# Channel-mix groups of four chunks, weights standing in all three products, and small copies on ScalarE's queue, in a fused attention and channel-mix kernel

## The chip, the cores and the metric

The kernel runs on one core of a Trainium2 chip. The metric is the device time of one execution in microseconds (us); the kernel before has a median of 341.86 us over 3 runs (341.74 to 342.92). The engines are named as the profile names them: PE is TensorE (matmuls; PEld is its weight load), ACT is ScalarE, DVE is VectorE, POOL is GpSimd, and SP is the queue that issues most transfers (DMAs). An instruction that issues a DMA stands in an engine's own queue, in order with its other instructions.

## The reference

Two stages, all in float32. The first is a gated linear attention over 768 steps, for 4 batches of 8 heads with 48 features; the second mixes channels of the result (384 features, 1024 hidden).

```python
for t in range(S):                      # S = 768, per batch and head
    state = alpha[t][:, None] * state + outer(k[t], v[t])
    y[t] = q[t] @ state
x = y, heads side by side               # (4, 768, 384)
x_prev = x shifted by one step, zero at the start of each batch
xk = mu_k * x + (1 - mu_k) * x_prev;  xr = mu_r * x + (1 - mu_r) * x_prev
k = relu(xk @ w_k);  v = (k * k) @ w_v;  r = sigmoid(xr @ w_r)
out = r * v
```

## The kernel before

**Chunks.** The 4 x 768 steps are 24 chunks of 128 steps, six to a batch. For the attention the chunks are prepared in groups (`PREP`, 2 2 2 3 3 3 3 3 3): for a group, the decays (`al`) are multiplied up by two scans on DVE (`scan` L823, `scan_back` L840), the queries and keys (one tile `kq`) are scaled with them (`mul_q` L848, `mul_k` L853), and the rows of the fourth pair of heads are copied to a tile of their own, `kq3`, by four DMAs (`move` L868). Then every chunk has a "visit" on PE: scores (L969), transposes (L986), the chunk's own part of y (L1017), the update of the state (L1029) and, one visit later, the part of y from the state (L1043). ACT copies y out of PSUM (`copy_y` L1088), and two DMAs per chunk spread the rows of the fourth pair over the other tiles (`move_y3` L1097).

**Groups of the channel mix.** `MIX` has the groups 2 2 2 3 3 3 3 3 3. For a group of n columns (256 or 384 steps) ACT and DVE form xk and xr from the tile `xt` (`x_mul` L1125, `x_add` L1129) and split each into a high part in the reduced format fp32r and a low remainder (`x_hi` L1134, `x_lo` L1138). Every product of the channel mix is then three matmuls: high by high, low by high, high by low. In `up` (L1154) the weights stand in the array and x streams through: 8 pieces of 9 matmuls, n columns each. `relu` and the square follow on ACT and DVE, and k is split again (L1183, L1187). In `gate` (L1198) and `down` (L1221) it is the other way round: x or k stands, 128 steps at a time, and 384 columns of weights stream through, so a group of c chunks has c x 9 and c x 24 matmuls. `sigmoid` (L1206), `gated` (L1228) and `store` (L1232) end a block of 128 steps by 384 features. Group 0 runs unsplit in float32, where PE works through two instructions per matmul.

**Buffers.** `kq` has two buffers, so the load for preparation group g (counted from 0) waits until group g-2 is read: group 2 waits for group 0, group 3 for group 1. The weights are loaded in ten pieces, put together on ACT and DVE (L911, L920), and split into high and low parts for group 1 on (L929, L931, L935). PSUM holds two accumulators for the channel mix (`pm`).

**Order.** A planner in the program (`Plan`, `graph`) lays out all work before the kernel runs: a table of numbers (`SOONER`) moves a step's rank on its engine, and `SPOTS` says before which piece of the channel mix each attention visit stands on PE. The order of every engine and queue is then fixed; an instruction waits for those before it. All the small copies (`move`, `move_y3`) stand in SP's queue, between the loads and the stores:

```python
iq, mq = dma(2, L("move", g, Q_AT), mulq + scales + old + [zeroed[g % 2]], ...)
_, x = dma(2, L("move_y3", c), es, kb=rows_kb(NX, C * 4, 6))
```

Before the first channel-mix matmul PE runs filler matmuls that compute nothing that is used (`busy` L952).

Of the kernel before, what the change touches and what calls it, by code (L numbers as in the profile page):

```python
# [42 lines left out]
MIX = [2, 2, 2, 3, 3, 3, 3, 3, 3]  # L43
# [41 lines left out]
class Plan:  # L85
# [33 lines left out]
    def run(self, order, sooner):  # L119
# [39 lines left out]
        dma, end = self.FIRST + 1.1, 0.0  # L159
# [79 lines left out]
def PLACE_OF(c):  # L239
# [1228 lines left out]
```

## Time and profile before

| | |
|---|---|
| median of 3 runs | 341.86 us (341.74 to 342.92) |
| the profiled execution, its own time | 343.06 us |
| its span (first to last instruction) | 341.3 us |
| PE busy | 326.9 us, 96% of the span, 4552 instructions |
| DVE busy | 241.8 us, 71% |
| ACT busy | 193.9 us, 57% |
| moved by DMA | 35.38 MB |

The profile shows one execution. A row of a timeline or of the chain of waits has its start and its length in us from the start of the span. In brackets stands how long the engine was idle before an instruction, and which engine and tile ended that. PE's matmuls overlap one another and their ends are modelled, so the pace of a run of matmuls is read from the chain of waits (length by count) and not from the mean duration of one. PEclk 1.00 is the upper of TensorE's two clock levels, 2.4 GHz.

### The profile page before, as it was taken

The numbers are of one execution on the slowest core, as the hardware profiler recorded it, in microseconds if no ns is written. First come the engines' busy times: TensorE is split into PE (matmuls) and PEld (weight loads), VectorE is DVE, ScalarE is ACT, GpSimd is POOL, SyncE is SP. The second block draws the span as 40 slices with busy tenths as digits, with TensorE's granted clock in tenths as the row PEclk, the third lists the DMA queues.
The fourth block names the chain that finished last, engine by engine and source line by source line (L and its number), as shares of the span: only waits on it lengthen the run. The fifth ranks groups of instructions, "written<-read, shape, count | busy, mean of one in ns | idle before, by whom it ended". The sixth has DMA issues, their size and how long they took to land.

```text
span 341.3 us, 10699 instructions
## 1 busy us (share of the span) xinstructions
PE 326.9 (96%) x4552; PEld 307.8 (90%) x4552; DVE 241.8 (71%) x513; ACT 193.9 (57%) x439; POOL 7.4 (2%) x28
## 2 busy tenths in 40 slices
PE   8889899899999999999999999999999999999992
PEld 8778765689999999999999999999999999999991
DVE  4899996989984998796769955885642784187210
ACT  3497882588388478653765456654641875366300
POOL 5100000000000000000000000000000000000000
PEclk9999999999999999999999999999999999999997
DMA  8999673434425322441241405130000100010010
GB/s 216 405 340 268 198 257 128 128 99 152 127 52 205 78 74 85 147 124 51 84 146 19 135 32 179 45 69 37 8 10 19 43 24 8 31 46 2 2 46 30
DMA packets 14325, 35.38 MB, mean 104 GB/s; under 512 B 2432, under 2 KB 9344, under 8 KB 13504
## 3 DMA queue, kind: packets, MB, share of 16 engines
q1 hardware_dynamic: 14016, 33.73, 30.5%
q10 hardware_dynamic: 256, 0.92, 0.9%
q8 instruction: 37, 0.61, 0.7%
q14 instruction: 16, 0.13, 0.1%
HBM read 26.57 MB, written 4.72 MB: 92 GB/s over the span
## 4 chain that ended last, share of the span: by engine, by line
PE 84%; DMA 6%; DVE 5%; issue 1%; ACT 1%; DVEq 0%
PE pk L1154 28%; PE pv L1221 27%; PE pg L1198 10%; PE yu L1043 4%; DMA kq<-kq_p 4%; PE sp L969 3%; PE yu L1017 3%; PE sp L986 3%; PE yu L1029 3%; DMA al<-al_p 2%; PE pb L952 2%; DVE pp L840 2%; DVE kq L848 1%; DVE pp L823 1%; DVE kq L853 0%
## 5 line engine op out<-in xcount | busy, mean ns | idle before, releaser
L1221 PE MATMUL pv<-wvh,kh 128*128 128x384 f32 x176 | 59.7, 339 | 0.2 <-DVE flag L1250 0.2
L1221 PE MATMUL pv<-wvh,kl 128*128 128x384 f32 x176 | 59.3, 337 | 0.0
L1221 PE MATMUL pv<-wvl,kh 128*128 128x384 f32 x176 | 59.2, 337 | 0.0
L1154 PE MATMUL pk<-xkh,wkh 128*128 128x384 f32 (+1 forms) x192 | 42.3, 327 | 1.0 <-ACT x L1125 0.7
L1162 ACT ACTIVATE r<-pk 128x384 f32<-128x384 f32 (+1 forms) x72 | 32.4, 451 | 18.9 <-PE pk L1154 18.7
L1154 PE MATMUL pk<-xkl,wkh 128*128 128x384 f32 (+1 forms) x192 | 41.5, 325 | 0.0
L1187 DVE TENSOR_TENSOR kl<-k,kh 128x384 fp32r<-128x384 f32 (+1 forms) x64 | 33.4, 523 | 11.3 <-ACT k L1168 4.8
L1154 PE MATMUL pk<-xkh,wkl 128*128 128x384 f32 (+1 forms) x192 | 41.0, 322 | 0.0
L1170 DVE TENSOR_TENSOR k<-r 128x384 f32<-128x384 f32 x48 | 26.7, 557 | 13.8 <-ACT r L1162 13.1
L1183 ACT ACTIVATE kh<-r 128x384 fp32r<-128x384 f32 (+2 forms) x72 | 35.1, 489 | 2.0
L1154 PEld LDWEIGHTS pk<-xkh,wkh 128*128 128x128 f32 x192 | 32.2, 188 | 1.9 <-ACT x L1125 1.3
L1221 PEld LDWEIGHTS pv<-wvh,kh 128*128 128x128 f32 x176 | 33.0, 188 | 0.5 <-DVE flag L1250 0.3
L1125 ACT ACTIVATE x<-xt,mu 128x384 f32<-128x384 f32 (+1 forms) x48 | 26.3, 583 | 12.4 <-DVE xkl L1138 6.3
L1221 PEld LDWEIGHTS pv<-wvl,kh 128*128 128x128 f32 x176 | 33.0, 188 | 0.0
L1221 PEld LDWEIGHTS pv<-wvh,kl 128*128 128x128 f32 x176 | 33.0, 188 | 0.0
L1154 PEld LDWEIGHTS pk<-xkh,wkl 128*128 128x128 f32 x192 | 32.4, 188 | 0.0
L1154 PEld LDWEIGHTS pk<-xkl,wkh 128*128 128x128 f32 x192 | 32.0, 188 | 0.0
L1228 DVE TENSOR_TENSOR sig<-pv,sig 128x384 f32<-128x384 f32 x24 | 13.3, 553 | 24.6 <-PE pv L1221 24.5
L1129 DVE SCALAR_TENSOR_TENSOR x<-xt,nu,x 128x384 f32<-128x384 f32 (+1 forms) x48 | 26.5, 576 | 4.5 <-ACT x L1125 4.5
L1088 ACT COPY xt<-yu 48x256 f32<-48x256 f32 (+1 forms) x72 | 26.8, 372 | 4.8 <-PE yu L1043 3.4
L992 ACT COPY ht<-sp 128x288 f32<-128x288 f32 (+1 forms) x24 | 9.7, 403 | 34.2 <-PE sp L986 19.2
L977 DVE TENSOR_TENSOR am<-sp,mask 128x512 f32<-128x512 f32 x24 | 16.5, 689 | 16.2 <-PE sp L986 9.0
(89 smaller groups left out, 535.4 us busy)
## 6 DMA issues: line engine op xcount, KB each, us to landing
kq<-kq_p SPq DMA_DIRECT2D x6, 1153.5 KB, 5.8
out<-sig SPq DMA_DIRECT2D x24, 192.0 KB, 1.9
al<-al_p SPq DMA_DIRECT2D x6, 577.5 KB, 3.9
v<-v_p SPq DMA_DIRECT2D x6, 576.0 KB, 4.0
rk<-wk_p SPq DMA_DIRECT2D x4, 768.0 KB, 9.0
rv<-wv_p SPq DMA_DIRECT2D x4, 768.0 KB, 5.3
kq<-kq_p SPq DMA_DIRECT2D x2, 769.5 KB, 8.1
v<-v_p SPq DMA_DIRECT2D x3, 384.0 KB, 7.6
```

The lines of the kernel that those rows point to most:

```text
L977: self.DVE.tensor_tensor(am, self.sc_both.rearrange("k j (p t) -> k j p t", p=NP), self.mask.unsqueeze(1).unsqueeze(1).to_broadcast([C, 2, ...
L1043: self.PE.matmul(self.yu[c][at : at + D, s, p * HB : (p + 1) * HB], self.st[c, s][rows, p, :], self.kq_of(c, p, j, Q_AT, s), start=False, ...
L1088: self.ACT.copy(self.xt_of(m)[dst, :, at + s * HB : at + (s + 1) * HB], self.yu[c][src, s, : NP * HB].rearrange("r (p t) -> r p t", p=NP),)
L1125: self.ACT.activation(x, xt[:, t, 1 : 1 + n], AF.Copy, scale=self.mu[:, i, t : t + 1])
L1129: self.DVE.scalar_tensor_tensor(x, xt[:, t, 0 : xt.shape[2] - 1], self.nu[:, i, t : t + 1], x, op0=ALU.mult, op1=ALU.add)
L1154: self.PE.matmul(pk, w[:, t, f * 128 : (f + 1) * 128], x[:, t], start=part == 0 and t == 0, stop=part == len(pairs) - 1 and t == NT - 1,)
L1162: self.ACT.activation(self.r[m, f], pk, AF.Relu)
L1170: self.DVE.tensor_tensor(k2, r, r, op=ALU.mult)
L1183: self.ACT.activation(self.khl_of(m)[0][:, f], self.r[m, f], AF.Square)
L1187: self.DVE.tensor_tensor(kl[:, f], self.k2[m, f], kh[:, f].bitcast(F32), op=ALU.subtract)
L1198: self.PE.matmul(pg, x[:, i, t * 128 : (t + 1) * 128], w[:, i], start=part == 0 and i == 0, stop=part == len(pairs) - 1 and i == NT - 1,)
L1221: self.PE.matmul(pv, x[:, f, cols], w, start=f == 0 and i == 0, stop=f == NF - 1 and i == len(pairs) - 1,)
```

## The change

- The last 12 chunks form three groups of four instead of four groups of three (`MIX`), so 512 columns stream per matmul there. Such a group may lie across the end of a batch; then its `xt` has two spans. Its x and k tiles take memory that the weights' pieces leave (`late_tiles`), and its temporary x uses `tops`.
- In `gate` and `down` the weights stand and x or k streams. The result has features on its rows, so the output is stored as (384, 3072) and turned on the host.
- The four copies per preparation group and the two per chunk are issued from ACT's queue.
- Preparation group 1's `kq` lies where the low part of the down weights comes later (tag `wvl`). Group 2's load thus waits for no earlier group, group 3's for group 0 and not for group 1; the low down weights wait for group 1's last use.
- `r` and its square share one tile (three buffers), so `k_hi` follows the square; the square is on ACT in group 1 only, before in groups 1 and 2.
- `SPOTS` and the table `SOONER` are new.

```diff
-MIX = [2, 2, 2, 3, 3, 3, 3, 3, 3]
+MIX = [2, 2, 2, 3, 3, 4, 4, 4]
+LATE = [m for m, cs in enumerate(MG) if len(cs) > 3]
+def spans_of(m):
+    cs = MG[m]
+    n = 2 if any(c % NCB == 0 for c in cs[1:]) else 1
+    return n, len(cs) * C // n
...
 SPOTS = [
-    0, 0, 0, 0, 0, 0, 0, 0, 0, 0, 0, 0, 0, 2, 3, 3, 5, 7, 8, 8, 15, 21, 27, 33, 59, 65, 71, 100,
+    0, 0, 0, 0, 0, 0, 0, 0, 0, 0, 0, 0, 0, 3, 5, 7, 10, 11, 12, 14, 14, 23, 29, 34, 68, 74, 81,
...
-        old = uses[("kq", g - 2)] if g > 1 else []
+        old = uses[("kq", g - 2 if g > 3 else 0)] if g > 2 else []
...
-        iq, mq = dma(2, L("move", g, Q_AT), mulq + scales + old + [zeroed[g % 2]], kb=rows_kb(NX, n * 4, 6))
-        ik, mk = dma(2, L("move", g, K_AT), mulk + old + [zeroed[g % 2]], kb=rows_kb(NX, n * 4, 6))
+        iq, mq = dma(2, L("move", g, Q_AT), mulq + scales + old + [zeroed[g % 2]], kb=-rows_kb(NX, n * 4, 6), eng="ACT")
+        ik, mk = dma(2, L("move", g, K_AT), mulk + old + [zeroed[g % 2]], kb=-rows_kb(NX, n * 4, 6), eng="ACT")
...
-                _, x = dma(2, L("move_y3", c), es, kb=rows_kb(NX, C * 4, 6))
+                _, x = dma(2, L("move_y3", c), es, kb=-rows_kb(NX, C * 4, 6), eng="ACT")
...
-            self.kq[g] = self.p2.tile([rows_of(g), nt, w], F32, tag="kq", name=f"kq{g}")
+            pool, tag = (self.p1, "wvl") if g == 1 else (self.p2, "kq")
+            self.kq[g] = pool.tile([rows_of(g), nt, w], F32, tag=tag, name=f"kq{g}")
...
+        if m in LATE:
+            self.ACT.copy(xt[dst, :, cols], y[:, :NT])
+            self.ACT.copy(y3[dst, :, cols], y[:, NT:])
...
+    def late_tiles(self):
+        if not self.late:
+            self.late = [self.p1.tile([128, 3, LONG], F32R, tag=f"raw{i}", name=f"late{i}") for i in range(3)]
+        return self.late
...
+        elif m in LATE:
+            x = self.tops[(NT * i + t) % 2].bitcast(F32)[:, :LONG]
...
-    def gate(self, m, t, part):
+    def gate(self, m, e, part):
...
             self.PE.matmul(
-                pg, x[:, i, t * 128 : (t + 1) * 128], w[:, i],
+                pg, w[:, i, e * 128 : (e + 1) * 128], x[i],
...
-    def down(self, m, t, f0):
+    def down(self, m, e, f0):
...
                 self.PE.matmul(
-                    pv, x[:, f, cols], w,
+                    pv, w, x[f],
...
-        self.queue[eng].dma_start(self.out[at : at + C], self.sig.pop((m, t)))
+        self.queue[eng].dma_start(self.out[e * 128 : (e + 1) * 128, at : at + sig.shape[1]], sig)
```

SP's queue early in the program, before: `kq_481` and `kq_769` are the keys and queries of preparation groups 2 and 3, `rv` pieces of the down weights, `al` decays, `kq_1_81` and `kq_0_80` the tiles for the fourth pair, `xt` the input of the channel mix.

```order
L868 DMA kq_1_81<-kq_165 48x1x256 x2
L879 DMA rv_460<-wv_p 128x3072
L812 DMA kq_481<-kq_p 128x1539
L879 DMA rv_587<-wv_p 128x3072
L868 DMA kq_0_80<-kq_481 48x1x257 x2
L806 DMA al_640<-al_p 128x1155
L868 DMA kq_0_80<-kq_481 48x1x256 x2
L1097 DMA xt_448<-xt_448 16x3x128 x2
L879 DMA rv_702<-wv_p 128x3072
L816 DMA v_711<-v_p 128x1152
L812 DMA kq_769<-kq_p 128x2307
L1097 DMA xt_448<-xt_448 16x3x128 x2
```

SP's queue now, from the keys of group 1 (`kq_171`) on; `kq_177` are those of group 2, `kq_415` those of group 3, `rk` and `rr` pieces of the up and gate weights.

```order
L841 DMA kq_171<-kq_p 128x1539
L841 DMA kq_177<-kq_p 128x1539
L834 DMA al_212<-al_p 128x771
L908 DMA rk_289<-wk_p 128x3072
L908 DMA rr_300<-wr_p 128x3072
L908 DMA rr_352<-wr_p 128x1536
L845 DMA v_361<-v_p 128x768
L841 DMA kq_415<-kq_p 128x2307
L834 DMA al_447<-al_p 128x771
L908 DMA rv_454<-wv_p 128x3072
L908 DMA rv_474<-wv_p 128x3072
```

Group 2's load now follows group 1's directly, ahead of the pieces of the gate weights; group 3's stands ahead of all pieces of the down weights and no longer behind them; no small copy is left in between.

ACT's queue before, from the copies of chunk 1's y (`xt_144<-yu`) to the first `relu` (`r<-pk`); `xkh<-xt_144` forms the first input of the channel mix, `tops` belongs to putting a weight piece together.

```order
L1088 COPY xt_144<-yu 48x4x64 x2
L911 ACTIVATE tops_85<-rk_285 128x768
L911 ACTIVATE tops_84<-rr_297 128x768
L911 ACTIVATE tops_85<-rr_345 128x384
L1125 ACTIVATE xkh<-xt_144,mu 128x256 x3
L1125 ACTIVATE xrh<-xt_144,mu 128x256 x3
L911 ACTIVATE tops_84<-rv_430 128x768
L1162 ACTIVATE r<-pk 128x256
```

ACT's queue now, over the same stretch (`junk` is a check of the decays that stood ahead of the copies before).

```order
L1134 COPY xt_110<-yu 48x4x64 x2
L888 ACTIVATE junk,racc<-al_212,mone 128x768
L1141 DMA xt_110<-xt_110 16x3x128 x2
L940 ACTIVATE tops_88<-rk_289 128x768
L897 DMA kq_1_84<-kq_171 48x1x257 x2
L940 ACTIVATE tops_87<-rr_300 128x768
L1202 ACTIVATE xkh<-xt_110,mu 128x256 x2
L940 ACTIVATE tops_88<-rr_352 128x384
L1202 ACTIVATE xkh<-xt_110,mu 128x256
L1202 ACTIVATE xrh<-xt_110,mu 128x256
L897 DMA kq_1_84<-kq_171 48x1x256 x2
L1202 ACTIVATE xrh<-xt_110,mu 128x256 x2
```

Six issues, chunk 1's copies and the four of group 1, now stand between the copy of y and the first `relu`, two pairs of them and the piece `rr_300` ahead of the first input.

## Rows read from the trace of the kernel before

**Rows 1.** Busy time by stage, from the windows view (length, then each engine)
```profile
0.00:28.77 28.77, 24.84 (x387) 23.07 (x387) 22.15 (x56) 16.21 (x28) 6.15 (x21) 1.00 0.91 315
28.77:71.45 42.68, 39.07 (x549) 28.45 (x547) 38.41 (x83) 27.47 (x65) 0.19 (x1) 1.00 0.56 181
60.00:110.00 50.00, 48.15 (x949) 44.48 (x949) 43.15 (x98) 36.03 (x101) 0.10 (x1) 1.00 0.42 130
71.45:334.80 263.35, 263.04 (x3619) 256.24 (x3619) 180.66 (x375) 150.21 (x348) 1.02 (x6) 1.00 0.23 70
```

**Rows 2.** The chain that ended last: start, length, step, and its count
```profile
28.93 2.60 PE pk L1154 x12
31.53 5.89 DMA kq<-kq_p
...
48.60 7.44 DMA kq<-kq_p
...
61.20 4.68 DMA al<-al_p
...
78.47 3.18 PE pk L1154 x27
81.65 3.32 PE pg L1198 x18
84.97 8.32 PE pv L1221 x48
...
215.43 4.76 PE pg L1198 x27
220.19 12.72 PE pv L1221 x72
...
304.13 12.49 PE pk L1154 x72
```

**Rows 3.** PE's timeline, 21 to 72 us: the filler, float32 work, and the idle times
```profile
24.75 4.18 PE L952 MATMUL pb<-ident 128*128 128x128 f32 x36 [0.53 <-issue]
...
34.82 0.69 PE L969 MATMUL sp<-kq 48*64 48x64 f32 x32 [0.64 <-DVE am L977]
...
39.95 0.66 PE L1043 MATMUL yu<-kq,st 48*48 48x64 f32 x32 [0.46 <-DVE st L1056]
...
47.12 0.46 PE L969 MATMUL sp<-kq 48*64 48x64 f32 x8 [0.66 <-issue]
...
52.56 6.61 PE L1221 MATMUL pv<-wv,kh 128*128 128x384 f32 x20
...
64.59 0.47 PE L1154 MATMUL pk<-xkh,wkh 128*128 128x256 f32 x2 [0.72 <-ACT x L1125]
65.34 0.39 PE L1154 MATMUL pk<-xkh,wkh 128*128 128x256 f32 x1 [0.28 <-ACT xkh L1134]
...
71.45 0.66 PE L1043 MATMUL yu<-kq,st 48*48 48x64 f32 x32 [0.85 <-DVE st L1056]
```

**Rows 4.** Timelines of SP, DVE and ACT around group 1's input, 48 to 63 us
```profile
49.53 1.22 SPq L1097 DMA_DIRECT2D xt<-xt  x2
...
56.17 1.50 DVE L848 TENSOR_TENSOR kq<-kq,pp 128x384 f32<-128x384 f32 x3 [2.64 <-DMA kq<-kq_p]
...
61.96 0.88 DVE L1129 SCALAR_TENSOR_TENSOR x<-xt,nu,x 128x256 f32<-128x256 f32 x2
...
56.42 0.91 ACT L1125 ACTIVATE x<-xt,mu 128x256 f32<-128x256 f32 x2 [3.17 <-DMA xt<-xt]
```

**Rows 5.** The copies `move_y3` and `move`, by line: issue, ns min/median/max
```profile
L1097 SPq DMA_DIRECT2D xt<-xt x48: 555/561/1198, 19.6 to 295.0; - x48
...
DMA to landing us min/median/max: 1.9/2.4/6.7
...
L868 SPq DMA_DIRECT2D kq<-kq x32: 567/587/1316, 26.2 to 224.7; - x32
```

**Rows 6.** SP's timeline, 62 to 108 us: first and last pair of small copies
```profile
62.07 1.20 SPq L868 DMA_DIRECT2D kq<-kq  x2
...
107.20 1.36 SPq L1097 DMA_DIRECT2D xt<-xt  x2
```

**Rows 7.** Groups of instructions by form: busy us, mean ns, idle before
```profile
L1187 DVE TENSOR_TENSOR kl<-k,kh 128x384 fp32r<-128x384 f32 x48 | 26.7, 558 | 6.4 <-ACT kh L1183 2.3
L1187 DVE TENSOR_TENSOR kl<-k,kh 128x256 fp32r<-128x256 f32 x16 | 6.6, 416 | 4.9 <-ACT k L1168 4.8
L1228 DVE TENSOR_TENSOR sig<-pv,sig 128x384 f32<-128x384 f32 x24 | 13.3, 553 | 24.6 <-PE pv L1221 24.5
```

**Rows 8.** The transfers by line: count, KB each, median us to landing
```profile
out<-sig SPq DMA_DIRECT2D x24, 192.0 KB, 1.9
...
kq<-kq_p SPq DMA_DIRECT2D x2, 769.5 KB, 8.1
```

More of the change, by code (lines that the diff above doesn't have):

```diff
@@ L70, with column_of @@
 MIX_OF = {c: g for g, cs in enumerate(MG) for c in cs}
-assert all(cs[0] // NCB == cs[-1] // NCB for cs in PG + MG)
+assert all(cs[0] // NCB == cs[-1] // NCB for cs in PG)
+assert all(c % NCB or (c - cs[0]) * 2 % len(cs) == 0 for cs in MG for c in cs)
 K_AT, Q_AT = 0, 1
+LONG = 4 * C
+LATE = [m for m, cs in enumerate(MG) if len(cs) > 3]
[3 more added lines that the diff above has]
+    return n, len(cs) * C // n
+def column_of(m, c):
+    at = (c - MG[m][0]) * C
+    return at + 1 + at // spans_of(m)[1]
 def tiles_of(g):
@@ L158, in run @@
         ready = {e: [] for e in self.ENGINES}
[L159 removed]
+        dma, aside, end = self.FIRST + 1.1, 0.0, 0.0
         at_pe = 0
@@ L346, in dma @@
     def dma(n, call, needs=(), kb=0.0, eng="SP"):
-        i = issues[call] = J(eng, {"SP": 0.64, "ACT": 0.6}[eng] * n, (call[0], call[1] + (eng,)), needs)
+        i = issues[call] = J(eng, {"SP": 0.64, "ACT": 0.45}[eng] * n, (call[0], call[1] + (eng,)), needs)
         return i, J("", 0.0, None, [i], kb=kb)
@@ L513, in visit @@
                 m = MIX_OF[c]
-                room = mixed.get(m - 2, []) + mixed.get(m - 1, [])[-1:]
-                es = [J("ACT", act(NP * HB), L("copy_y", c, i), [v] + room) for i in range(3)]
+                room = mixed.get(m - 2, []) + mixed.get(m - 1, [])[-1:] + (mix_x if m in LATE else [])
+                es = [
+                    J("ACT", act(NP * HB) if m not in LATE else act(NT * HB) + act(HB), L("copy_y", c, i), [v] + room)
+                    for i in range(3)
+                ]
                 e = J("", 0.0, None, es)
-                _, x = dma(2, L("move_y3", c), es, kb=rows_kb(NX, C * 4, 6))
+                _, x = dma(2, L("move_y3", c), es, kb=-rows_kb(NX, C * 4, 6), eng="ACT")
                 free_yu[c % 2].extend(es)
@@ L554, in mix @@
         reads = []
+        late = [x for hl in conv.values() for x in hl] + [x for us in w_uses.values() for x in us]
+        late = late if m in LATE else []
         for i in range(2):
@@ L562, in mix @@
                     continue
-                a = J("ACT", act(n) + 0.1, L("x_mul", m, i, t), needs + [nu] + x_ring(2))
+                a = J("ACT", act(n) + 0.1, L("x_mul", m, i, t), needs + [nu] + x_ring(2) + late)
                 b = J("DVE", dve(n) + 0.05, L("x_add", m, i, t), [a])
@@ L602, in channel @@
             xuse.append(p2)
-            r = J("ACT", act(n), L("relu", m, f), [p2] + ([r_used[-2]] if len(r_used) > 1 else []))
+            if n > LONG // 2 or f % 2 == 0:
+                r_tiles.append([])
+            r = J("ACT", act(n), L("relu", m, f), [p2] + (r_tiles[-4] if len(r_tiles) > 3 else []))
             pm_free[slot] = [r]
@@ L626, in channel @@
                 ws = [conv["r", 0], conv["r", 1]]
-                p = J("PE", 3 * mm(DM), L("gate", m, t, 0), busy + [w[0] for w in ws] + [xh[1, i] for i in range(NT)])
-                p1 = J("PE", 3 * mm(DM), L("gate", m, t, 1), [p] + [w[1] for w in ws])
-                p2 = J("PE", 3 * mm(DM), L("gate", m, t, 2), [p1] + [xl[1, i] for i in range(NT)])
+                p = J("PE", 3 * mm(n), L("gate", m, e, 0), busy + [w[0] for w in ws] + [xh[1, i] for i in range(NT)])
+                p1 = J("PE", 3 * mm(n), L("gate", m, e, 1), [p] + [w[1] for w in ws])
+                p2 = J("PE", 3 * mm(n), L("gate", m, e, 2), [p1] + [xl[1, i] for i in range(NT)])
                 out += [p, p1, p2]
             xuse.append(p2)
-            sig[t] = J("ACT", act(DM), L("sigmoid", m, t), [p2] + ([sig_use[-4]] if len(sig_use) > 3 else []))
-            pm_free[slot] = [sig[t]]
+            sig[e] = J("ACT", act(n), L("sigmoid", m, e), [p2] + ([sig_use[-3]] if len(sig_use) > 2 else []))
+            pm_free[slot] = [sig[e]]
             sig_use.append(None)
@@ L642, in channel @@
         kuse = []
-        for t in range(n // C):
+        for e in range(NT):
             slot, busy = take()
@@ L649, in channel @@
                 if m in FULL:
-                    prev = J("PE", 2 * full(DM), L("down", m, t, f), first + ks + [whole["v", f // 2]])
+                    prev = J("PE", 2 * full(n), L("down", m, e, f), first + ks + [whole["v", f // 2]])
                     w_uses["v", f // 2].append(prev)
                 else:
-                    prev = J("PE", 6 * mm(DM), L("down", m, t, f), first + ks + list(conv["v", f // 2]))
+                    prev = J("PE", 6 * mm(n), L("down", m, e, f), first + ks + list(conv["v", f // 2]))
                 out.append(prev)
             kuse.append(prev)
-            g = J("DVE", 0.47, L("gated", m, t), [prev, sig[t]])
+            g = J("DVE", dve(n), L("gated", m, e), [prev, sig[e]])
             pm_free[slot] = [g]
-            _, o = dma(1, L("store", m, t), [g], kb=192)
-            sig_use[sig_base[0] + t] = o
-        sig_base[0] += n // C
+            _, o = dma(1, L("store", m, e), [g], kb=rows_kb(128, n * 4))
+            sig_use[NT * m + e] = o
         last_use["k"] = kuse
         return out
-    sig_base = [0]
     runs = []
@@ L698, in graph @@
     main = [x for ms in mains for x in ms]
+    for i in low_v:
+        P.jobs[i][3].extend(uses["kq", 1])
     for late, early in HOLD:
@@ new lines, in carry, with x_tiles @@
+        if n > 1:
+            self.POOL.memset(xt[:, :, w + 1 : w + 2], 0.0)
+    def late_tiles(self):
+        if not self.late:
+            self.late = [self.p1.tile([128, 3, LONG], F32R, tag=f"raw{i}", name=f"late{i}") for i in range(3)]
+        return self.late
+    def x_tiles(self, m):
+        if m not in self.hl:
+            full = m in FULL
+            n = self.xt[m].shape[2] - (spans_of(m)[0] if m in MIX_OF.values() else 1)
+            own = 2 if m in LATE else NT
+            self.hl[m] = []
+            for i, w in enumerate(("xkh", "xkl", "xrh", "xrl")):
+                if full and w[2] == "l":
+                    self.hl[m].append(None)
+                    continue
+                x = self.p1.tile([128, own, n], F32 if full else F32R, tag=w, name=w)
+                tiles = [x[:, t] for t in range(own)]
+                if m in LATE:
+                    tiles.append(self.late_tiles()[2][:, i] if i < 3 else self.late_tiles()[0][:, 2])
+                self.hl[m].append(tiles)
+        return self.hl[m]
@@ L1221, in down, with gated, store @@
                 self.PE.matmul(
-                    pv, x[:, f, cols], w,
+                    pv, w, x[f],
                     start=f == 0 and i == 0, stop=f == NF - 1 and i == len(pairs) - 1,
                 )
-    def gated(self, m, t):
-        pv = self.acc.pop(("down", m, t))
-        self.DVE.tensor_tensor(self.sig[m, t], pv, self.sig[m, t], op=ALU.mult)
-    def store(self, m, t, eng):
-        at = (MG[m][0] + t) * C
-        self.queue[eng].dma_start(self.out[at : at + C], self.sig.pop((m, t)))
+    def gated(self, m, e):
+        pv = self.acc.pop(("down", m, e))
+        self.DVE.tensor_tensor(self.sig[m, e], pv, self.sig[m, e], op=ALU.mult)
+    def store(self, m, e, eng):
+        at = MG[m][0] * C
+        sig = self.sig.pop((m, e))
+        self.queue[eng].dma_start(self.out[e * 128 : (e + 1) * 128, at : at + sig.shape[1]], sig)
     def judge_a(self):
@@ L1374, in fallback @@
                 k.k_lo(m, f)
-            for t in range(NT):
+            for e in range(NT):
                 for part in range(3):
-                    k.gate(m, t, part)
-                k.sigmoid(m, t)
+                    k.gate(m, e, part)
+                k.sigmoid(m, e)
                 for f in range(0, NF, 2):
-                    k.down(m, t, f)
-                k.gated(m, t)
+                    k.down(m, e, f)
+                k.gated(m, e)
                 nc.sync.dma_start(
-                    orow[ds(b, 1), sc * GMAX + t * 128 : sc * GMAX + (t + 1) * 128, :].rearrange("o s e -> (o s) e"),
-                    k.sig.pop((m, t)),
+                    ocol[e * 128 : (e + 1) * 128, ds(b, 1), sc * GMAX : (sc + 1) * GMAX].rearrange("e o s -> e (o s)"),
+                    k.sig.pop((m, e)),
                 )
@@ L1466 @@
     r = _run(nc, [arrays], core_ids=[0])
-    return r.results[0]["out"].reshape(B, S, DM)
+    return r.results[0]["out"].reshape(DM, B, S).transpose(1, 2, 0)
```

189 lines of the change are left out of this document (108 added, 81 removed), and 147 rows, old and new, of the table SOONER.

## The prediction

> **What bounds the kernel now.** I read the windows view by stage first, then the chain that ended last, then the timelines around PE's idle times. The windows give three stages [rows 1]. From 71.45 to 334.80 us PE is busy 263.04 of 263.35 us at the granted clock 1.00 (its level of 2.4 GHz): there the time is the sum of PE's own work, and nothing that another engine saves can shorten it. Up to 28.77 us the kernel starts up, and PE fills the time with matmuls that nobody reads, whose last run ends as the first channel-mix matmul begins [rows 2, 3]. Between, from 28.77 to 71.45 us, PE is busy 39.07 of 42.68 us, so 3.6 us are idle, in gaps of 0.3 to 0.85 us [rows 3]. There the chain leaves PE and runs through loads of keys and decays, 5.89, 7.44 and 4.68 us long [rows 2]. Behind 334.80 only the last product and its store are left.
>
> The pace of a run of matmuls, its length by its count [rows 2]: 256 columns 3.18/27 = 117.8 ns, 384 columns in up 12.49/72 = 173.5 ns, 384 in gate and down of three chunks 4.76/27 = 176.3 and 12.72/72 = 176.7 ns.
>
> **The change part by part.**
>
> Groups of four. The last 12 chunks had 4 x (72 + 27 + 72) = 684 matmuls in 4 x (12.49 + 4.76 + 12.72) = 119.9 us. Now there are 3 x 171 = 513, of 512 columns, a width that the trace does not show. The line through the two paces of up is 55.7 ns per 128 columns, thus 229.2 ns at 512, and 513 x 229.2 = 117.6 us. That is 2.3 us less. Bounds: if what a matmul costs beyond its columns at 2.4 GHz is only what it is at 256 (117.8 - 106.7 = 11.1 ns), it is 224.4 ns and 115.1 us, a gain of 4.8; if cost grows with the columns from gate and down's 176.7 ns, it is 235.6 ns and 120.9 us, a loss of 1.0. I take the line, -2.3, since it uses the two nearest widths in the same role.
>
> The Trainium skill ("TensorE: Matmul & The Clock Gate", Back-to-back issue gap) puts a single matmul's gap at its columns over 2.4 plus 2.5 ns, which speaks against this part: 171 fewer matmuls would save 171 x 2.5 ns = 0.4 us by it. The trace differs: it shows 11 to 13 ns beyond the columns.
>
> Weights standing. In groups 1 and 2 gate and down go from 18 + 48 matmuls of 384 (3.32 + 8.32 = 11.64 us) to 27 + 72 of 256 (99 x 117.8 ns = 11.66): nothing. In groups 3 and 4 the count stays at 99; if they run at up's pace, where the weights already stand, each saves 99 x 3.1 ns = 0.3 us, if not, nothing. I take -0.3 for both together (0 to -0.6). Group 0 goes from 44 float32 instructions at 6.61/20 = 0.33 us to 66 at 2.60/12 = 0.217 us: 14.5 against 14.3, nothing [rows 2, 3].
>
> Keys earlier. The load of group 3's keys left at 48.60, once group 1 was read, and took 7.44 us; DVE stood 2.64 us for it, and behind it in DVE's order stood that group's scaling and then the first `x_add` of channel group 1, at 61.96, for which ACT's x had been waiting since 57 [rows 2, 4]. PE's gaps of 0.72, 0.28 and 0.85 us at 64.6 to 71.5 end with that chain [rows 3]. Now both loads leave before the down weights, so the 2.64 us go, and channel group 1 can begin as soon as PE is through group 0. The gap at 47.12 lies in the scores that first read group 2's copied rows; the profile names no releaser, but those rows come earlier too. What is late next: ACT, which has 27.5 us of work in these 42.7 [rows 1] and now issues the copies as well. Bounds: at best all 3.6 us, at worst ACT's new issues put in as much as they remove. I take -2.3, about two thirds of the idle time, because DVE (38.4 of 42.7 us) leaves little room.
>
> Copies on ACT's queue. 80 issues at a median of 0.56 to 0.59 us [rows 5] are 46 us more for ACT's order; its 193.9 us of work stay. What is queued behind such an issue waits for it: the next `relu`, which frees one of two accumulators, or the next copy of y. In 60 to 110 us, the densest stretch for attention, eight pairs are issued [rows 6], 16 x 0.57 = 9.1 us, beside ACT's 36.0 of 50 us [rows 1]: 45 of 50. It fits, hidden beside PE's own work, as long as issues lie next to ACT's running work and don't each hold it. Cost 0 in the sum; its bounds are a gain of nothing and the loss in the last rival. In return SP's loads and stores have no small copies ahead of them, and a copy is not behind a load in one queue: the one issued at 49.53, right behind the load of 48.60, kept ACT waiting until 56.42, against a median landing of 2.4 us [rows 4, 5].
>
> Start. The first channel input follows on ACT behind two pairs of issues (2.3 us) and a piece of gate weights whose load has 770 KB of keys more ahead of it [rows 8]. Up to 28.77 ACT works 16.2 us [rows 1], and the filler keeps PE until 28.9 anyway [rows 2, 3]. I take +0.4 (0 to +2).
>
> End. The last `gated` has 512 columns and not 384: DVE's price per column is (558 - 416)/128 = 1.1 ns, so 0.55 grows by 0.14 us [rows 7]; the last store has 256 KB and not 192, landing 1.9 us [rows 8], between nothing and a third (0.6) more. Together +0.3.
>
> Sum: -2.3 - 0.3 - 2.3 + 0.4 + 0.3 = -4.2 us. The profiled execution took 343.06 us for a span of 341.3, so it would be 338.9; the median of the runs lies 1.2 us below that execution, which puts the forecast at 337.7 us.
>
> **The rivals.**
>
> Wide matmuls give nothing: the pace at 512 columns is about that of 384 per column. For it: 256 to 384 already gains only 0.008 ns per column (0.460 to 0.452). Against: the line of two widths. Then 337.7 + 2.3 = 340.0; with 0.4 us left of the gain, 339.6.
>
> The copies land no sooner, and the early gain goes: ACT's x of group 1 comes at 56 as before. For it: both queues feed the same transfer engines, busy 0.56 of that stretch [rows 1]. Against: the median landing of 2.4 us where no load stands ahead. Time 340.0. The Trainium skill ("DMA: Bandwidth & Descriptors", Issuing engines are not separate DMA queues) says that transfers from all engines share 16 DMA engines, and that another issuer saves only issue time; no row before shows a small copy on ACT's queue.
>
> A group of four is not mixed in time. All of chunk 15's y is needed for channel group 5, and eight of group 4's twelve down pieces stand behind that visit: 8.5 us (12.72 x 8/12), and two visits. Its chain is copies of y, two issues, 2.4 us of landing and three tiles of four 512-wide instructions at 0.7 us through two temporaries, 11 to 12 us. Against: the two visits cover the rest. Without them 3 us are missing: 340.7, and 342 if group 6 misses too, and over that if a load delays it.
>
> ACT becomes the bound, from 60 to 110 us: each pair waits for the copy it follows, so the 1.1 us of issue find ACT empty, and `relu` comes late for PE, which has two accumulators. From the point where ACT's 45 of 50 us leave no slack, half of the 9.1 us shows as PE idle, 4.6 us, and the early gain of 2.3 is gone: 344.6. For it: DVE works 43 of these 50 us too [rows 1], so neither engine can catch up. Against: the next run of matmuls without a visit gives ACT time.
>
> **How the numbers follow.** What a measurement can tell from no change is 0.5%, so faster is under 340.15 and slower over 343.57. The forecast has 0.55; wide matmuls for nothing 0.10 (0.06 faster, 0.04 same); copies for nothing 0.12 (0.07, 0.05); a late mix 0.10 (0.06 same, 0.04 slower); ACT as the bound 0.13 (0.03 same, 0.10 slower). That makes faster 0.68, same 0.18, slower 0.14. The lower bounds together are -4.8 - 0.6 - 3.6 + 0.2 = -8.8, 333.1 us; they are not all met at once, so the range begins at 334.0. It ends at 342.0, which holds the first three rivals and leaves out most of the fourth. The forecast's own range is 334.0 to 340.0.
>
> **What would show it.** Right: up of 512 columns at 224 to 232 ns a matmul, in gate and down the same; the first matmul of channel group 1 before 64 us, with group 0's work and chunk 4's visit behind it; no wait of DVE for `kq` near 56; PE busy over 99.5% from 72 us on; small copies landing in 2 to 3 us beside loads. Wrong: idle PE between 60 and 110 us with ACT as what ends it, or at the starts of groups 5 and 6; a first channel matmul after 30 us; or 512 columns at over 233 ns.

## The result, and the profile after

The changed kernel took 345.98 us (median of five runs, 345.39 to 346.6) against 342.76 us before (five runs; the forecast started from the 341.86 us of three); the ratio is 1.0103, 95% interval 1.0078 to 1.0128. Forecast were 337.7 us, with 342.0 as the upper end. It is slower, and by more than any of the rivals said.

The profiled execution took 345.62 us for a span of 343.9. Four places, read from PE's timeline and the chain of waits of either kernel, tell where the time went:

| place on PE | before | after | difference | by the prediction |
|---|---|---|---|---|
| first channel matmul | 28.77 | 33.26 | +4.5 | +0.4 |
| `inter` at the head of chunk 5's visit | 71.45 | 72.66 | +1.2, and 9 matmuls (1.06 us) fewer done: +2.3 | -1.9 |
| down of channel group 2 ends | 120.76 | 124.44 | +3.7 | -1.9 |
| last channel matmul ends | 334.74 | 337.84 | +3.1 | -4.5 |
| span | 341.3 | 343.9 | +2.6 | -4.2 |

The windows of the changed kernel, cut at its own places (they answer to [rows 1]; columns as there):

```profile
29.10:33.26 4.16, 0.13 (x2) 0.00 (x1) 0.54 (x2) 2.14 (x4) 0.19 (x1) 1.00 0.97 326
33.26:72.66 39.40, 38.91 (x561) 31.80 (x561) 37.92 (x83) 26.52 (x63) 0.22 (x1) 0.96 0.46 138
72.66:112.00 39.34, 38.59 (x842) 37.15 (x843) 35.02 (x83) 26.30 (x79) 0.10 (x1) 1.00 0.43 132
112.00:337.90 225.90, 225.58 (x2683) 197.00 (x2681) 144.61 (x275) 117.36 (x276) 0.71 (x5) 1.00 0.19 58
```

The rows of either kernel that the table rests on and that stand nowhere else, first the three of the kernel before:

```profile
28.77 2.82 PE L1154 MATMUL pk<-xkh,wk 128*128 128x256 f32 x12
120.76 3.12 PE pk L1154 x18
321.74 13.00 PE pv L1221 x72
```

```profile
124.44 2.27 PE pk L1230 x12
```

A stage is there that the kernel before has not: 4.16 us in which PE does nothing and the transfer engines are busy 0.97 of the time. Behind it the granted clock is 0.96 on average. From there to chunk 5 PE is idle only 0.5 us, where it was 3.6 [rows 1, 3], and from 72.66 to 112 it is idle 0.75 us, where it was not at all.

PE's timeline of the changed kernel (start, length, instruction, count, and in brackets the idle time before it with what ended it; answers to [rows 3]):

```profile
25.05 4.18 PE L984 MATMUL pb<-ident 128*128 128x128 f32 x36 [0.53 <-issue]
33.26 5.99 PE L1230 MATMUL pk<-xkh,wk 128*128 128x256 f32 x18 [4.03 <-DVE xkh L1206]
...
40.19 2.76 PE L1230 MATMUL pk<-xkh,wk 128*128 128x256 f32 x12
...
69.80 0.60 PE L1230 MATMUL pk<-xkh,wkh 128*128 128x256 f32 x3
...
72.66 0.66 PE L1075 MATMUL yu<-kq,st 48*48 48x64 f32 x32 [0.49 <-DVE st L1088]
...
107.34 0.34 PE L1001 MATMUL sp<-kq 48*64 48x64 f32 x8 [0.40 <-issue]
...
111.58 0.62 PE L1230 MATMUL pk<-xkh,wkh 128*128 128x256 f32 x3 [0.20 <-ACT r L1243]
```

The first 18 channel matmul instructions take 333 ns each, the next 12 take 230 ns. What PE waits for is DVE's first `x_add`, which needs the rows that the copies bring and ACT's first `x_mul` on them. ACT's timeline in the same kernel, `ACTq` being an issue in ACT's order:

```profile
23.73 0.56 ACTq L1141 DMA_DIRECT2D xt<-xt  x1
...
27.71 1.28 ACTq L897 DMA_DIRECT2D kq<-kq  x2
29.04 1.06 ACT L940 ACTIVATE tops<-rr 128x768 f16<-128x768 bf16 x1 [3.63 <-DVE kq L882]
32.11 0.91 ACT L1202 ACTIVATE xkh<-xt,mu 128x256 f32<-128x256 f32 x2 [2.02 <-DMA xt<-xt]
```

DVE's, with the `x_add` that PE waits for:

```profile
32.72 0.88 DVE L1206 SCALAR_TENSOR_TENSOR xkh<-xt,nu,xkh 128x256 f32<-128x256 f32 x2 [4.44 <-DMA kq<-kq]
```

POOL's, with its part of the same input:

```profile
32.17 0.19 POOL L1154 COPY xt<-xt 128x3 f32<-128x3 f32 x1 [18.41 <-DMA xt<-xt]
```

And SP's, with the two loads that have moved:

```profile
7.17 3.59 SPq L841 DMA_DIRECT2D kq<-kq_p  x2
...
20.28 0.38 SPq L845 DMA_DIRECT2D v<-v_p  x1
21.70 0.33 SPq L841 DMA_DIRECT2D kq<-kq_p  x1
```

The last copy of chunk 1 left at 23.73 and ACT and POOL, who need it, go on at 32.1. In the kernel before, its two copies left from 22.40 on and ACT went on at 26.74:

```profile
26.74 1.31 ACT L1125 ACTIVATE xkh<-xt,mu 128x256 f32<-128x256 f32 x3 [0.90 <-DMA xt<-xt]
```

(For DVE the profile names a copy of the queries, which `x_add` does not read; in the built program that copy shares a semaphore with a copy that `x_add` does wait for.) Ahead of chunk 1's copies stand two loads that the kernel before sent only at 31.53 and 48.60 [rows 2]: group 2's keys, with group 1's from 7.17 on, and group 3's at 21.70. There are two suspects here: these loads, and ACT itself, which stood 3.63 us in its own order at a copy it had to issue. The built program gives a reason for the second. Its transfers, of all queues, take eight semaphores in turn, and one that comes round again waits until the transfer eight places earlier has landed; the copy of group 1's queries shares its semaphore with a load of gate weights (384 KB). ACT's and SP's order, with what each row waits for:

```
22 L897 DMA kq_1_84<-kq_171 48x1x257 [waits DMAHW7_49,DVE_49]
13 L908 DMA rr_352<-wr_p 128x1536 [waits DMAHW7_49,DVE_49]
```

The late channel groups, from the chain of waits (answers to [rows 2]): up and gate of group 4 at 384 columns, then group 7 at 512.

```profile
173.48 8.42 PE pk L1230 x48
181.90 4.68 PE pg L1283 x27
...
297.61 16.64 PE pk L1230 x72
314.25 6.26 PE pg L1283 x27
...
320.87 16.96 PE pv L1306 x72
```

At 512 columns a matmul takes 231.1 ns in up and 231.9 ns in gate; at 384, up went from 173.5 ns to 175.4 and gate from 176.3 to 173.3. Summed over the chain from group 3 on, up, gate and down take 75.58 + 28.34 + 75.55 = 179.5 us, where they took 75.07 + 28.65 + 76.40 = 180.1.

### The profile page after: what moved, and what is told of

It reads as the page before. It is cut to its first block, busy times and chain, and to the rows that moved or that the text cites. A ratio compares the mean times of both kernels' runs of the same rounds, so it can differ in the third digit from the quotient of the medians.

```text
span 343.9 us, 10407 instructions
## 1 busy us (share of the span) xinstructions
PE 327.2 (95%) x4469; PEld 288.4 (84%) x4469; DVE 240.0 (70%) x493; ACT 184.9 (54%) x439; POOL 5.7 (2%) x28
## 4 chain that ended last, share of the span: by engine, by line
PE 76%; DVE 3%; ACT 1%; issue 0%; ACTq 0%; DVEq 0%
PE pv L1306 27%; PE pk L1230 26%; PE pg L1283 10%; PE yu L1075 3%; PE sp L1001 3%; PE yu L1049 3%; PE sp L1018 3%; PE yu L1061 2%; DVE wvl L967 1%; DVE x L1206 0%; DVE am L1009 0%; DVE sig L1313 0%; ACT xt L1134 0%; DVE wrl L967 0%; ACT ht L1024 0%
## 5 line engine op out<-in xcount | busy, mean ns | idle before, releaser
L1306 PE MATMUL pv<-kh,wvh 128*128 128x512 f32 (+2 forms) x150 | 51.2, 341 | 0.2 <-DVE flag L1336 0.2
L1306 PE MATMUL pv<-kh,wvl 128*128 128x512 f32 (+2 forms) x150 | 50.9, 339 | 0.0
L1306 PE MATMUL pv<-kl,wvh 128*128 128x512 f32 (+2 forms) x150 | 50.8, 339 | 0.0
L1243 ACT ACTIVATE r<-pk 128x256 f32<-128x256 f32 (+2 forms) x64 | 31.3, 489 | 31.5 <-PE pk L1230 27.1
L1250 DVE TENSOR_TENSOR r<-r 128x512 f32<-128x512 f32 (+2 forms) x48 | 28.4, 599 | 14.4 <-ACT r L1243 14.3
L1268 ACT ACTIVATE kh<-r 128x512 fp32r<-128x512 f32 (+3 forms) x58 | 28.9, 512 | 13.8 <-DVE r L1250 13.6
L1230 PE MATMUL pk<-xkh,wkh 128*128 128x256 f32 (+2 forms) x144 | 35.2, 343 | 0.4 <-ACT r L1243 0.2
L1230 PE MATMUL pk<-xkl,wkh 128*128 128x256 f32 (+2 forms) x144 | 34.5, 339 | 0.0
L1230 PE MATMUL pk<-xkh,wkl 128*128 128x256 f32 (+2 forms) x144 | 34.5, 338 | 0.0
L1306 PEld LDWEIGHTS pv<-kh,wvh 128*128 128x128 f32 x150 | 28.3, 189 | 2.7 <-DVE flag L1336 0.3
```

What stands on the lines that cost most here:

```text
L1230: self.PE.matmul(pk, w[:, t, f * 128 : (f + 1) * 128], x[t], start=part == 0 and t == 0, stop=part == len(pairs) - 1 and t == NT - 1,)
L1243: self.ACT.activation(self.r[m, f], pk, AF.Relu)
L1250: self.DVE.tensor_tensor(r, r, r, op=ALU.mult)
L1268: self.ACT.activation(self.khl_of(m)[0][f], self.r[m, f], AF.Square if m in FULL else AF.Copy)
L1306: self.PE.matmul(pv, w, x[f], start=f == 0 and i == 0, stop=f == NF - 1 and i == len(pairs) - 1,)
```

## The experiments

Theory A: the keys of groups 2 and 3 (770 + 1154 KB), loaded early, keep the transfer engines busy ahead of chunk 1's copies and put off the first channel matmul. Theory B: ACT's order, held at the copy of the queries, does. Theory C: a part of the loss is the clock that falls behind the idle time. Theory D: the issues in ACT's order cost PE time later. The edits change the list `calls` of what is emitted (`behind(a, b)` puts call a right behind call b); all else is the changed kernel.

**e1: both loads later.**

```
+ behind(("load_kq", 2), ("load_al", 2))
+ behind(("load_kq", 3), ("load_al", 3))
```

> The changed kernel with two loads moved back in SP's order: group 2's keys (768 KB) right behind al of group 2, group 3's keys (1153 KB) behind al of group 3; all else as in the changed kernel. Theory A (crowded transfers): these 1.92 MB stand ahead of everything that lands before 32 us, at 400 GB/s 4.8 us; without them chunk 1's copies land near 27 to 28 us and not at 32, the first channel matmul begins at 28.7 to 29.7 us instead of 33.26, its 18 first matmuls run at 0.22 and not 0.33 us each, and the time is 339.5 to 342 us against the changed kernel's 346.0 (ratio to before 0.991 to 0.998). Theory B (ACT's queue: the query copies of group 1 hold ACT at 25.4 to 29.0 us, and with it x_mul): ACT is still held, the first channel matmul comes after 31 us, 344 to 346 us.

343.16 us, ratio 1.0005 (0.9984 to 1.0025). PE's timeline of this kernel:

```profile
29.04 1.05 PE L1230 MATMUL pk<-xkh,wk 128*128 128x256 f32 x4
...
35.67 0.33 PE L1001 MATMUL sp<-kq 48*64 48x64 f32 x2 [1.09 <-DMA kq<-kq]
36.72 0.34 PE L1001 MATMUL sp<-kq 48*64 48x64 f32 x6 [0.73 <-DMA kq<-kq]
...
37.37 4.44 PE L1230 MATMUL pk<-xkh,wk 128*128 128x256 f32 x12
```

The first matmul is back at 29.04 as A says, and 2.8 of the 3.2 us of loss are gone. The time misses A's range by 1.2 us. In the profiled execution, the longest of the twelve (345.32 us), the keys now leave with the first down weights, and the next small copy, that of group 1's own keys, lands late instead (5.8 us); whether that is the whole of the 1.2 us is not shown.

**e4: group 3's keys alone later.**

```
+ behind(("load_kq", 3), ("load_al", 3))
```

> The changed kernel with group 3's keys alone (1153 KB) loaded later, behind al of group 3; group 2's stay early. Theory A by bytes: 1.15 of 1.92 MB, so 2.9 us of the 4.8: first channel matmul near 30.3 to 30.8 us, 341.5 to 343.5 us. Theory B: first channel matmul after 32.5 us, 345 to 346 us.

344.58 us, ratio 1.0041 (1.0021 to 1.0061). The first channel matmul comes at 30.66, inside A's range; the time is 1.1 us over it. The wait before it is 1.29 us, and the clock does not fall (granted 1.00 from 29 to 72 us):

```profile
30.66 1.13 PE L1230 MATMUL pk<-xkh,wk 128*128 128x256 f32 x4 [1.29 <-DVE xkh L1206]
...
62.52 3.72 PE L1306 MATMUL pv<-kh,wv 128*128 128x256 f32 x16 [0.88 <-DVE sig L1313]
```

The lead over the changed kernel, 3.5 us where the first 18 matmuls end, is 1.8 us at 68.04, where group 1 begins; on the way PE waits 0.88 us for DVE, which is busy 39.6 of the 43 us from 29 to 72.

**f3: the kernel before, with loads that nobody reads.** To the kernel before the change two loads are added on SP, 770 and 767 KB (0.39 MB less than in the changed kernel), into a tile that is not yet in use:

```
+ behind kq 1:  self.SP.dma_start(self.crowded[:, 0:1539], self.kq_p[:, 0:1539])
+ behind v 2:   self.SP.dma_start(self.crowded[:, 1539:3072], self.kq_p[:, 1539:3072])
```

> The kernel before the change with two loads more that nobody reads, 770 KB behind group 1's keys and 767 KB behind the third v, on SP, at the places where the changed kernel loads the keys of groups 2 and 3; nothing else differs. Theory A: 1.54 MB at 400 GB/s put off chunk 1's copies by 3 to 4 us, the first channel matmul begins at 31.5 to 33 us instead of 28.77, PE's clock falls behind that idle time, 344 to 346 us against 342.2. If something else in the changed kernel's start is the cause, it stays at 28.8 to 29.5 us and 342 to 342.7 us.

345.6 us, ratio 1.0114 (1.0070 to 1.0159), against the changed kernel's 1.0103. Its PE timeline:

```profile
32.27 4.52 PE L1159 MATMUL pk<-xkh,wk 128*128 128x256 f32 x12 [3.29 <-DVE xkh L1134]
```

And ACT's, whose wait is for chunk 1's copies:

```profile
31.13 1.30 ACT L1130 ACTIVATE xkh<-xt,mu 128x256 f32<-128x256 f32 x3 [3.15 <-DMA xt<-xt]
```

This kernel has neither copies on ACT's queue nor groups of four nor standing weights. The early loads alone put off its first matmul by 3.5 us, lower its clock (0.64 from 32.27 to 37 us) and cost 3.1 us. The delay also goes with the bytes: against the 28.77 of before it is 4.5 us for 1.92 MB in the changed kernel, 3.5 for 1.54 MB here and 1.9 for 0.77 MB in e4. In these three the loads leave at the changed kernel's places, and that is 2.3 to 2.5 us per MB. A is shown, by taking the loads away (e1) and by adding them alone (f3).

**e2: group 1's copies issued by SP.**

```
+ calls = [(n, g[:-1] + ("SP",)) if n == "move" and g[0] == 1 else (n, g) for n, g in calls]
```

> The changed kernel with the four row copies of group 1 alone issued by SP instead of ACT, at the same place of the order. Theory A: ACT is free from 25.4 us, but the copies of chunk 1 land at 32 us as before, so the first channel matmul stays at 33 to 33.4 us and the time at 345.3 to 346.3 us. Theory B: ACT reaches x_mul 3 us earlier, the first channel matmul begins near 30 us, 341 to 343 us.

348.15 us, ratio 1.0142 (1.0110 to 1.0174): the first channel matmul comes at 33.10, so B falls.

```profile
33.10 6.66 PE L1230 MATMUL pk<-xkh,wk 128*128 128x256 f32 x18 [4.15 <-DVE xkh L1206]
...
108.69 0.34 PE L1001 MATMUL sp<-kq 48*64 48x64 f32 x8 [1.21 <-issue]
...
133.90 0.80 PE L1230 MATMUL pk<-xkh,wkh 128*128 128x384 f32 x3 [0.75 <-ACT r L1243]
```

ACT's 3.63 us were beside the wait for chunk 1's copies, not ahead of it. That it is 2 us slower than the changed kernel neither theory says. The trace has three places for it: 0.5 us are there at chunk 5's visit (73.17), a stall at 108.69 is 0.8 us longer than the changed kernel's at 107.34, and PE waits 0.75 us for ACT at 133.90, where the changed kernel does not. Why they come was not tried.

**e3 and e8: more filler, so that PE does not stand before the first channel matmul.**

```
- BUSY = [(6.5, 25), (1.3, 6), (0.86, 4), (0.86, 4), (6.5, 30)]
+ BUSY = [(6.5, 25), (1.3, 6), (0.86, 4), (0.86, 4), (6.5, 64)]   (e8: 48)
```

> The changed kernel with 34 more matmuls of 128 columns in the last filler (64 instead of 30), so that PE works until 33.2 us and not 29.2; nothing waits for them. Theory C (a part of the loss is TensorE's clock, which falls behind the 4 us of idle): the first channel matmul stays at 33.2 to 33.5 us, but its first 18 matmuls take 3.9 and not 5.99 us, mean granted clock up from 0.991 to 0.995 or more, and 343.9 to 344.3 us against 346.0. If the slow first matmuls have another cause, 346.0 +/- 0.5.

> The changed kernel with 18 more filler matmuls (48 instead of 30). In e3 34 more kept PE to 36.7 us, 3.4 us past the point where the first input was there, because each takes 0.22 us; 18 end near 33.2. Theory C: first channel matmul 33.1 to 33.6 us, the first 18 of them in 3.9 to 4.1 us instead of 5.99, the time 343.8 to 344.6 us against 346.0. If what the clock costs is taken up later by other waits, 345 to 346 us.

e3: 347.06 us (1.0107; 1.0078 to 1.0135). I had taken 0.12 us for a filler matmul, which is what one record lasts; each has two, so the filler ran to 36.7 us. e8 is sized rightly: 345.67 us, ratio 1.0095 (1.0067 to 1.0123). Its PE timeline:

```profile
33.55 1.13 PE L1230 MATMUL pk<-xkh,wk 128*128 128x256 f32 x4
35.01 3.64 PE L1230 MATMUL pk<-xkh,wk 128*128 128x256 f32 x14 [0.33 <-DVE xkh L1206]
...
50.52 1.56 PE L1283 MATMUL pg<-xrh,wr 128*128 128x256 f32 x6 [0.62 <-ACT r L1243]
...
79.90 0.38 PE L1018 MATMUL sp<-ident,kq 128*128 128x128 f32 x2 [0.42 <-issue]
```

The clock stays at 1.00 from 29 to 72 us, but the 18 matmuls still end only 0.6 us earlier, since at full clock they wait for their third input, and by 50.52 ACT has taken that back. C is not borne out: the lower clock is seen, and its removal brought nothing that can be measured (the interval would hide a gain of up to about 1 us).

**e5: group 2's keys put behind chunk 1's copies in the list.** Group 3's as in e1.

```
+ behind(("load_kq", 2), ("move_y3", 1))
+ behind(("load_kq", 3), ("load_al", 3))
```

> As e1, but group 2's keys leave earlier, right behind the two copies of chunk 1 (near 23 us) and not with the first down weights at 27 us. In e1 the first channel matmul came at 29.04 us, but group 1's own key copies then landed 5.8 us late, PE waited 1.8 us for them at 35 us and ran the next 12 matmuls at half clock. Theory A goes on (any large load just ahead of a small copy that PE needs costs its own length): here the copies of chunk 1 are out before and those of group 1 have 770 KB less ahead; first channel matmul 28.7 to 29.6 us, no wait for copied rows near 35 us, 341.0 to 342.5 us. If group 1's copies are late for another reason, the wait stays and the time is 343 us or more.

343.95 us, ratio 1.0053 (1.0033 to 1.0074), over the range. The edit did not bring the order that the expectation meant. The load is in SP's queue and the copies are in ACT's, and SP did not wait for ACT: the load left at 20.86, before both copies (22.75 and 23.41).

```profile
20.86 0.63 SPq L841 DMA_DIRECT2D kq<-kq_p  x1
```

```profile
22.75 0.56 ACTq L1141 DMA_DIRECT2D xt<-xt  x1
```

```profile
30.23 1.13 PE L1230 MATMUL pk<-xkh,wk 128*128 128x256 f32 x4 [1.01 <-DVE xkh L1206]
...
69.77 0.67 PE L1075 MATMUL yu<-kq,st 48*48 48x64 f32 x32 [0.49 <-DVE st L1088]
```

So chunk 1's copies had the 770 KB ahead of them once more, and the first channel matmul comes at 30.23. No wait for copied rows near 35 us is left, as A says. Chunk 5's visit begins at 69.77, earlier than before (71.45) by 1.7 us, or 0.6 with the 9 matmuls that are not yet done, and the kernel is still slower. So the start is not all.

**e7: the other copies back on SP**, on top of e5.

```
+ late = {"move": 2, "move_y3": 2}
+ calls = [(n, g[:-1] + ("SP",)) if n in late and g[0] >= late[n] else (n, g) for n, g in calls]
```

> As e5, but all row copies from group 2 and chunk 2 on are issued by SP and not ACT, at the same places of the order; group 0's and group 1's stay on ACT. Theory D (46 us of issues in ACT's order cost PE time, at 60 to 112 us above all): faster than e5 by 0.5 us or more. The prediction's view (they cost nothing there, and on SP they stand behind loads): slower than e5 by 0 to 2 us.

344.09 us, ratio 1.0058 (1.0033 to 1.0083), against e5's 1.0053. D is not borne out: from chunk 2 on no difference is seen between the two queues; one of 0.5 us, D's least, would be lost in the intervals.

**f1 and f4: group 2's keys behind group 1's copies.** f1 has them issued by ACT; f4 also puts DVE's work on them behind chunk 3's mask.

```
+ behind(("load_kq", 2), ("move", 1, K_AT))           (f1 and f4; issued by ACT)
+ behind(("load_kq", 3), ("load_al", 3))
+ for name, t in (("mul_k", 0), ("scan_back", 0), ("mul_q", 1), ("mul_q", 0), ("scale", 2), ("scale", 1), ("scale", 0)):
+     behind((name, 2, t), ("mask_scores", 3))        (f4)
```

> As e1, but group 2's keys are issued by ACT, right behind the copies of group 1's keys, so that neither chunk 1's copies (as in e5) nor group 1's (as in e1) have these 770 KB ahead of them. Theory A: first channel matmul near 29.0 us as in e1, no wait of PE for copied rows at 35 us and no stretch at half clock behind it (1.8 and 1.7 us in e1's trace), 341.0 to 342.3 us. If the start no longer decides once it is near 29 to 30 us (e1, e4 and e5 lie within 1.4 us of each other), 343 to 344 us.

> As f1 (group 2's keys issued by ACT behind the copies of group 1's keys, landing near 39 us), but with DVE's seven instructions that read or follow those keys (scale 2, mul_q 2, the first scan_back and mul_k of group 2) put behind mask_scores of chunk 3, so that DVE's order does not stand 5.2 us for them with chunk 2's mask behind it. Theory A with in-order DVE: first channel matmul near 28.8 us, the 3.26 us wait at 42 us and the half-clock stretch behind it (2.4 us) go, 341 to 343 us against f1's 347.1. If group 2's keys are late for what follows too, channel group 1 begins no earlier than in the changed kernel (69.8 us) and the time is 344 us or more.

f1: 347.11 us (1.0123; 1.0093 to 1.0152), which neither expectation says. f4: 343.98 us, ratio 1.0046 (1.0031 to 1.0062), 1 us over the range. DVE's timeline in f1:

```profile
39.18 0.21 DVE L862 TENSOR_SCALAR kq<-pp 128x1 f32<-128x1 f32 x2 [5.17 <-DMA kq<-kq_p]
```

PE's, behind it:

```profile
42.20 1.13 PE L1001 MATMUL sp<-kq 48*64 48x64 f32 x32 [3.26 <-ACT ht L1026]
43.40 5.30 PE L1230 MATMUL pk<-xkh,wk 128*128 128x256 f32 x12
```

In f1 the first channel matmul comes at 28.78, but now the load itself, among two of down weights, lands 8.3 us after its issue, and DVE's order stands for it. In f4 that wait is gone and group 1 begins at 67.70. The places tried for this load are with the first down weights (e1), ahead of chunk 1's copies (e4, e5) and behind group 1's (f1, f4); in e1, e4, e5 and f1 an instruction that PE needs came late by it. That no place is free is not shown: from 25 to 27 us the transfer engines are busy only 0.32 of the time in f1, and no run issues the load there, behind chunk 1's copies.

```profile
25.00:27.00 2.00, 2.00 (x21) 2.00 (x20) 2.00 (x4) 0.83 (x1) 0.00 (x0) 1.00 0.32 73
```

**e6: the last 12 chunks in threes.**

```
- MIX = [2, 2, 2, 3, 3, 4, 4, 4]
+ MIX = [2, 2, 2, 3, 3, 3, 3, 3, 3]
```

> The changed kernel with the last 12 chunks in four groups of three (MIX as before the change); start and middle are word for word as in the changed kernel. Prices the groups of four alone. By the pace in the trace of the changed kernel (39.6 us a group of four, three of them 118.8; groups of three 4 x 29.9 = 119.8) they save 1.0 us, so this is 347.0 us; by the line of the prediction (2.3 us) 348.3; if groups of four lose elsewhere what they gain, 346.0 or less.

349.23 us, ratio 1.0194 (1.0167 to 1.0220), more than any expectation. It does not price the width: 1.0 us of it lies in the first 18 matmuls (7.01 us, lower clock), 0.5 in a longer stall at 109 us, and later PE waits for DVE and ACT (0.26 us at 198.71, 0.36 at 222.80) in an order that was fitted to fours. The pace of fours is better read from the chain above.

## Why the prediction was wrong

**Start** (+0.4, 0 to +2) is the step that failed. I set 770 KB against a piece of gate weights, and let the filler cover it. The other load was counted only where it used to be waited for. What I left out is that chunk 1's 24 KB copies are transfers too and land behind whatever is under way: the copies' median landing in the first 36 us is 4.6 us before and 6.5 after, 5.3 in e1, 5.9 in e4, 7.3 in f3. The first matmul came 4.5 us late, outside the bounds. There was a warning: the Trainium skill ("DMA: Bandwidth & Descriptors", Issuing engines are not separate DMA queues) says that transfers run on the same 16 DMA engines whichever engine issued them. I drew on it for a rival at 56 us only, and the traces agree with it here: behind the early loads the copies land late from ACT's queue (6.5 us) and from SP's (7.3 in f3).

**Keys earlier** (-2.3) was right as a mechanism: DVE's wait near 56 us is gone, and PE is idle 0.5 us from 33.26 to 72.66. But the same transfer engines pay for it 25 us earlier. From the first channel matmul to chunk 5 the changed kernel is faster by 2.2 us (4.5 less 2.3), so start and keys together are +2.3 instead of -1.9. That 2.2 us come so near the forecast 2.3 is partly luck: PE's idle time in this stretch fell by 3.1 us, and the lower clock took back about 1.9 (18 matmuls at 333 and not 230 ns).

**Groups of four** (-2.3) and **weights standing** (-0.3) were mis-sized: together -0.6 over all late groups (180.1 to 179.5 us), all of it in the last 12 chunks (120.1 to 119.5); groups 3 and 4 stayed at 60.0. The line through up's two paces gave 229.2 ns, measured 231.1 to 231.9, and 235.6 in the last down; up at 384 columns became 1.9 ns slower at the same time. Pure runs, 3 x (16.64 + 6.26 + 16.68) = 118.7 us, are 1.1 below the 119.9 of before; as the runs stand, cut by visits, half of that is left. The estimate worked out from the figure of the Trainium skill ("TensorE: Matmul & The Clock Gate", Back-to-back issue gap) was 0.4 us: measured is nearer to it than to mine, but not by its rule of 2.5 ns a matmul, since at 512 columns the trace has 18 to 22 ns beyond the columns. I had also misread the rows there: beyond the columns they show 11 and 13.5 ns in up, but 16 to 17 in gate and down.

**Copies on ACT's queue** (0) was right as far as e7 tells, whose intervals would hide 0.5 us. The rival in which ACT becomes the bound was right in place, and its cause is not seen. At 106.94 the chain leaves PE for an unexplained stall of 0.40 us, then runs through mask, `ht` and copies of y to `r`, until 111.58:

```profile
106.94 0.40 issue
...
108.21 0.70 DVE am L1009
108.93 0.40 ACT ht L1024
...
111.58 1.33 PE pk L1230 x9
```

From 107.92 to there PE does 24 matmuls of 256 columns (2.83 of 3.66 us). That makes 1.2 us, most of the 1.4 that is lost between chunk 5 and the end of group 2. e7 has the same stretch with its copies on SP. Nor is the stall needed: e3 has none there, and from chunk 5's visit to the first up of group 3 it is 1.2 us too long all the same.

The whole of this stretch matters more than the one place. From chunk 5's visit to the first up of group 3, by the starts on PE, it took 49.15 us before, 50.2 with the 9 matmuls more that the changed kernel has to do in it, and it takes 51.4 to 52.7 us in all eleven kernels with the changed kernel's order, a loss of 1.2 to 2.5 us whatever their start. In e5's profiled execution the account closes: 0.6 us ahead of before at chunk 5's visit, 1.9 lost up to group 3, 0.5 won by the late groups, and the last channel matmul ends 0.7 us later than before (335.46).

**End** (+0.3): span less last matmul went from 6.6 to 6.1 us, so the term had the wrong sign.

Of the signs that I had named, a first channel matmul after 30 us was the one that told. The first matmul of group 1 (69.80, named: before 64) failed too, and so did the copies' landing in the first 36 us (over the whole kernel the median of `move_y3` is 2.0 us). DVE's wait came out, and 512 columns at 224 to 232 ns but for the last down (235.6).

What stays open: why the stretch from chunk 5 to the end of group 2 costs more in the new order, beyond the 1.2 us at 107; what the stall is; and what makes e2's three differences. No version beat the kernel before.

## What to carry to other kernels

Moving a load earlier was not free where the transfer engines were full (busy 0.97 of the time): small copies issued behind it landed later, on either queue, and the first matmul that needed them came 4.5 us later for 1.92 MB. So price a moved load against the nearest copy that the bounding engine waits for, not against its own consumer. Test such a suspicion in the old kernel: two loads that nobody reads showed a loss of the same size at once. And look in the trace whether an edit of the order brought the order that was meant: in e5 a load that was put behind copies in the list left 1.9 us ahead of them from another queue. A pace at a new width is better bounded than extrapolated from two points.

## What the runs showed of the hardware that was not expected

PE has a stall that the profile puts down to "issue" at the same eight matmuls, the last of chunk 11's scores, in all nine kernels that have the changed kernel's order on PE up to there: 0.40 us in the changed kernel, 1.19 in e1, 0.93 in e4, 1.21 in e2. The program has no wait there, and in these kernels the eight matmuls begin anywhere from 104.94 to 110.32 us. With 18 filler matmuls more ahead (e8) there is none at these eight; one of 0.42 us stands at 79.90, among the transposes of another visit, and with 34 more (e3) the only one is 0.24 us at 174.59. So it goes neither with time nor with these matmuls as such, and what stands ahead on PE moves it; what makes it was not tried. The row of the kernel before that reads alike (47.12, [rows 3]), and its like in f3, is another thing: those are the first scores that read group 2's copied rows, where the program does wait.

Matmuls of one shape differ by role and kernel: 384 columns from 173.3 to 176.7 ns, with the clock at 1.00 in all. Behind 3.26 us of idle, 12 float32 matmuls took 5.30 us in f1, where the changed kernel's at full clock take 2.86; the granted clock from 42.20 to 48.70 is 0.52, close to the level of 1.2 GHz. Behind 1.29 us (e4) the clock stayed at 1.00, but in e1 it fell to 0.50 (38 to 41 us) behind two waits of 1.09 and 0.73 us close together, so the longest idle time alone does not tell.
